# Dilated attention heads in three tiles of 128 partitions, with the instruction list drawn up anew

## The chip, the cores and the metric

The kernel runs on one core of a Trainium2 chip. The metric is the device time of one execution in microseconds (us). The engines are TensorE (PE; its weight loads are PEld), VectorE (DVE), ScalarE (ACT), GpSimd (POOL) and SyncE (SP, which issues all DMAs here).

## What is computed

Attention with eight heads of 64, four of them over a plain window of 32 keys and four over a dilated one (every fourth key, 32 of them), and on its result a feed-forward layer of 512 -> 2048 -> 512 with a gate. Cut to what matters:

```python
# q, k, v: (8, 8, 576, 64); w_in: (512, 2048), w_out: (2048, 512) in float64
rel = pos[:, None] - pos[None, :]
mask_plain = (rel >= 0) & (rel < 32)                        # heads 0 to 3
mask_dil = (rel >= 0) & (rel < 128) & (rel % 4 == 0)        # heads 4 to 7
scores = np.where(mask, q @ k.T / 8, -1e9)
attn = softmax(scores)
x = (attn @ v)                                              # -> (4608, 512)
h = x @ w_in
g = h * np.tanh(softplus(h))
return g @ w_out
```

## The kernel before

**Units.** The work is cut into 16 units of 288 tokens, half a sequence each (`u`, with `half`). A unit has two kinds of heads: kind 0 is plain, kind 1 dilated. Queries go in blocks of 32. Of kind 0 there are three tiles (`NB[0]`) of three blocks on 96 partitions (`QB`). Of kind 1 every residue modulo 4 has 72 queries, covered by three overlapping blocks, so there are four tiles of three blocks, one per residue. Keys of a block lie in a window of 64 (`WK`) or, in the first half of a sequence, 56 (`WD`).

**Steps of one unit.** `ld` loads q and keys, `qp` spreads the plain q on GpSimd, `lv` loads v (its dilated part `vd` in two or three transfers per half, each of which waits on SP for the one before), `sp` computes scores in PSUM (L577), `sc` masks and subtracts the row maximum on DVE (L598, L600, L609), `ex` is the exponential on ACT, `tp` splits the weights into two f16 parts and transposes them, `pr` finds the scale of v and splits it, `va` multiplies with v (L689), takes the denominators (`den`, ACT), their reciprocals (`rec`, DVE) and the quotient `xs` (L705), and `tx` splits `xs` into two f16 parts and transposes it into `x`. `va` and `tx` have three parts in a unit: 0 is kind 0, 1 and 2 are two tiles each of kind 1. Units 0 to 2 (`direct`) put the mask on by a matmul (L565) and transpose on PE (L659, L738); the others take a mask tile in SBUF and transpose by DMA.

**Feed-forward.** `ff` is the first product (L790, 128x288 matmuls, three passes of high and low parts), `gt`, `gq` and `ga` build the gated operand, `fo` (L972, units 0 to 2) and `fq` (L933, seven products instead of eight) are the second one.

**Weights.** They come as 64-bit numbers. `wl` loads a piece of 2 x 512 KB (ring `raw` of four buffers), `wm` copies the high words, `ww` makes f32 of the two words (POOL L411, DVE L413 and L415), `ws` finds the scale (PE L382 or L385, DVE), `wp` splits into two f16 parts (ACT L422, DVE L424). There are eight pieces of each matrix. `kw` and `kh` are matmuls on ones that fill PE early on.

**What sets the order.** The list `ORDER` is written out: each name calls the next part of a step, and its instructions are put on their engines in that order; `=n` names the PSUM buffer. Each engine runs its instructions in order, and SP its DMA issues. The small matmuls of the scores go round three column strips of 32 (`s`) and two row halves of 64 (`h`):

```python
        for t in range(nb):
            for a in range(2):
                for s in range(NS):
...
                    for h in range(2):
...
                        nc.tensor.matmul(pt[s * SQ:(s + 1) * SQ, h, c:c + w], q[hs, q0:q0 + SQ], d["k"][kind][hs, k0:k0 + w],
```

## Time and profile before

| | us |
|---|---|
| median of three runs | 858.7 (857.71 to 860.95) |
| the profiled execution | 862.81 |
| its span, first to last instruction | 860.9 |
| PE busy | 842.1 |
| DVE busy | 636.1 |
| ACT busy | 477.8 |
| POOL busy | 96.0 |

The page gives each engine's busy time as a share of the span. Matmuls are pipelined and their ends are modelled, so what a stretch of matmuls costs is read from the start of its first to the start of the next line. [...]

### The profile page before, as it was taken

To read this page: it belongs to the slowest core of one execution; us is meant where nothing else is said; L and a number is where in the kernel's file an instruction comes from. 1 tells how busy PE (TensorE), PEld (TensorE's weight loads), DVE (VectorE), ACT (ScalarE), POOL (GpSimd) and SP (SyncE) were. 2 spreads that over 40 slices of the span, in tenths; PEclk is the share of its full clock that TensorE was granted. 3 is DMA by queue.
4 is the path that set the end of the run, shared out by engine and by line. 5 is a ranking of instruction groups with operands and counts; after the bars stand their busy time and mean duration, and the time that the engine had idled before them with its cause. 6 is when DMAs were issued, how large, how long until landed. Compare 5 with 4: busy or idle time off the path is not lost.

```text
span 860.9 us, 32197 instructions
## 1 busy us (share of the span) xinstructions
PE 842.1 (98%) x14818; PEld 727.3 (84%) x14821; DVE 636.1 (74%) x818; ACT 477.8 (55%) x615; POOL 96.0 (11%) x99
## 2 busy tenths in 40 slices
PE   8798999999999999999999999999999999999998
PEld 7486777788788998988999889988889889988898
DVE  3788998586999897968777587977878764854353
ACT  2464655453486558765753775766446656624342
POOL 5116583210010001000000000010000000000000
PEclk9989999999999999999999999999999999999999
DMA  8648543366320437253623373725335160421001
GB/s 270 213 151 266 154 146 87 73 144 130 70 57 13 126 80 178 57 144 96 126 67 102 69 150 76 131 72 102 94 73 109 43 127 18 57 40 34 1 22 37
DMA packets 154887, 86.29 MB, mean 100 GB/s; under 512 B 92288, under 2 KB 150656, under 8 KB 154752
## 3 DMA queue, kind: packets, MB, share of 16 engines
q1 hardware_dynamic: 154752, 84.24, 40.9%
q8 instruction: 116, 1.90, 1.0%
q14 instruction: 19, 0.16, 0.1%
HBM read 56.89 MB, written 9.44 MB: 77 GB/s over the span
## 4 chain that ended last, share of the span: by engine, by line
PE 86%; DMA 7%; DVE 3%; SPq 2%; ACT 1%; issue 1%; POOL 0%; DVEq 0%; POOLq 0%; ACTq 0%
PE b L790 40%; PE b L933 31%; PE b L972 8%; DMA vf<-in_vd 4%; PE b L689 4%; PE b L577 3%; DMA raw<-in_w_in 2%; DMA knd<-in_kdT 1%; DVE g L903 1%; SPq L348 1%; DVE hm L909 0%; DVE w L424 0%; SPq L501 0%; PE b L385 0%; ACT g L901 0%
## 5 line engine op out<-in xcount | busy, mean ns | idle before, releaser
L790 PE MATMUL b<-x,w 128*128 128x288 f16 x3072 | 393.4, 286 | 0.2 <-ACT hm L796 0.2
L790 PEld LDWEIGHTS <-w 128*128 128x128 f16 x3072 | 295.4, 98 | 75.5 <-issue 0.6
L903 DVE SCALAR_TENSOR_TENSOR g<-hm,sg,g 128x1152 f16<-128x1152 f32 (+1 forms) x104 | 131.3, 1272 | 53.7 <-ACT g L901 52.9
L933 PE MATMUL b<-g,w 128*128 128x144 f16 x2496 | 164.9, 226 | 0.8 <-issue 0.7
L933 PEld LDWEIGHTS <-w 128*128 128x128 f16 x2496 | 158.4, 98 | 3.2 <-issue 1.1
L796 ACT ACTIVATE hm<-b,fs 128x576 f32<-128x576 f32 x128 | 92.8, 738 | 113.5 <-PE b L790 99.2
L901 ACT ACTIVATE g<-hm,sg 128x1152 f16<-128x1152 f32 (+1 forms) x104 | 116.0, 1127 | 40.1 <-PE b L933 26.4
L481 POOL COPY qp<-qn 128x576 f32<-128x576 f32 x15 | 34.9, 2326 | 433.6 <-DMA qn<-in_qT 317.9
L909 DVE TENSOR_TENSOR hm<-hm 128x576 f32<-128x576 f32 x104 | 79.0, 763 | 1.9 <-ACT hm L796 0.4
L972 PE MATMUL b<-g,w 128*128 128x288 f16 x576 | 73.3, 286 | 0.1
L947 ACT ACTIVATE y<-b,fo 128x288 f32<-128x288 f32 x52 | 40.6, 786 | 58.9 <-PE b L933 57.6
L972 PEld LDWEIGHTS <-w 128*128 128x128 f16 x576 | 55.6, 98 | 14.4 <-DVE w L424 0.3
L952 DVE SCALAR_TENSOR_TENSOR y<-b,fo,y 128x144 f32<-128x144 f32 x78 | 33.6, 478 | 45.8 <-PE b L933 22.7
L933 PE MATMUL b<-g,g 128*128 128x144 f16 x936 | 66.6, 226 | 0.3 <-DVE y L952 0.2
L933 PE MATMUL b<-g,late_sums 128*128 128x144 f16 x936 | 65.9, 226 | 0.0
L933 PEld LDWEIGHTS <-g 128*128 128x128 f16 x936 | 60.6, 98 | 2.2 <-issue 0.6
L933 PEld LDWEIGHTS <-late_sums 128*128 128x128 f16 x936 | 60.0, 98 | 0.5
L727 ACT CAST x<-xs 96x512 f16<-96x512 f32 (+1 forms) x39 | 26.7, 686 | 30.9 <-DMA x<-x 17.1
L729 DVE TENSOR_TENSOR x<-xs,x 96x512 f16<-96x512 f32 (+1 forms) x39 | 30.1, 772 | 16.6 <-ACT x L727 16.4
L545 DVE SCALAR_TENSOR_TENSOR vh<-vn,s,vh 128x2688 f16<-128x2688 f32 (+1 forms) x13 | 35.2, 2705 | 8.6 <-ACT vh L543 8.6
L705 DVE TENSOR_TENSOR xs<-b,rec 96x512 f32<-96x512 f32 (+1 forms) x48 | 37.2, 776 | 4.4 <-DVE rec L703 0.5
L689 PEld LDWEIGHTS <-pT 64*32 64x32 f16 (+1 forms) x3276 | 30.2, 90 | 5.3 <-issue 3.6
(127 smaller groups left out, 821.1 us busy)
## 6 DMA issues: line engine op xcount, KB each, us to landing
qn<-in_qT SPq DMA_DIRECT2D x15, 576.0 KB, 5.3
vn<-in_vd SPq DMA_DIRECT2D x66, 128.0 KB, 3.8
raw<-in_w_out SPq DMA_DIRECT2D x16, 512.0 KB, 5.2
out_T<-y SPq DMA_DIRECT2D x26, 288.0 KB, 2.8
raw<-in_w_in SPq DMA_DIRECT2D x12, 512.0 KB, 7.4
vn<-in_v SPq DMA_DIRECT2D x14, 288.0 KB, 4.2
knd<-in_kdT SPq DMA_DIRECT2D x14, 224.0 KB, 4.7
vn<-in_v SPq DMA_DIRECT2D x12, 256.0 KB, 3.7
```

The costliest lines, as they stand in the source:

```text
L481: nc.gpsimd.tensor_copy(qp.rearrange("p (b r i) -> p b r i", r=NR, i=SQ // NR), d["q"][:, :2 * HT].rearrange("p (b i r) -> p b r i", r=NR, ...
L545: nc.vector.scalar_tensor_tensor(lo, src, s, hi, ALU.mult, ALU.subtract)
L689: nc.tensor.matmul(avv[s * SQ:(s + 1) * SQ, a, t - t0, h * (D + 1):(h + 1) * (D + 1)], p, vv[vi][ks, v0:v0 + D + 1], start=(i == 0), stop= ...
L705: nc.vector.tensor_tensor(xs.rearrange("p (a t h e) -> p a t h e", a=2, h=2, e=D), avv[:, :, :, 1:AW - 1].rearrange("p a t (h e) -> p a t ...
L790: nc.tensor.matmul(ph[:, h, :HT], w1[j][:, c, wi, k * P:(k + 1) * P], x_of(d, xi, c), start=(n == 0), stop=(n == len(seq) - 1))
L796: nc.scalar.activation(d["m"][p][:, half, k0:k0 + 2], ph[:, :, :HT], AF.Mish, scale=d["fs"][:, j:j + 1])
L901: nc.scalar.activation(hi, src, AF.Identity, scale=sg)
L903: nc.vector.scalar_tensor_tensor(lo, src, sg, hi, ALU.mult, ALU.subtract)
L909: nc.vector.tensor_tensor(a, a, b, op=op)
L933: nc.tensor.matmul(acc[e], left(l, e, p, wi)[:, k * P:(k + 1) * P], right(gi, k), start=(n in opens and p == 0 and q == 0), stop=(last and ...
L947: nc.scalar.activation(into(half, t), by(acc), AF.Identity, scale=fo)
L972: nc.tensor.matmul(po[:, :HT], w2[:, e, j, wi, k * P:(k + 1) * P], d["g"][j][:, gi, k, :], start=(j == 0 and n == 0), stop=(j == NCH - 1 a ...
```

## The change

The dilated blocks are counted through all residues: block `j` of tile `t` is number `4 t + j`, and three tiles of four blocks lie on 128 partitions (`QS` is the number of rows of a tile, `NB` becomes 3 and 3). All rows of kind 1 then have 768 or 672 columns instead of 1024 or 896. `va` and `tx` have two parts in a unit, one per kind, so there is one `den`, `rec`, `xs`, one split and one transpose of kind 1 where there were two. The masks of kind 1 in units 3 to 15 come from SBUF tiles that `masks_late` makes by three more matmuls, since the pattern of a tile now differs from tile to tile; in units 0 to 2 the mask matmul is made per tile. GpSimd converts the weight words as before. The list `ORDER` is another one throughout (2030 names instead of 2123).

```diff
-    NB = (NPB, NR)
+    NB = (NPB, NR * NS * SQ // P)
+    QS = (QB, P)
...
+    def block(kind, t, j):
+
+        return divmod(t * P // SQ + j, NS) if kind else (t, j)
...
-                for s in range(NS):
-                    k0 = a * (NR * d["kd"] if kind else d["kw"]) + key_of(d, kind, t, s)
+                for j in range(nq // SQ):
+                    r, s = block(kind, t, j)
+                    k0 = a * (NR * d["kd"] if kind else d["kw"]) + key_of(d, kind, r, s)
...
-        src = pt[:QB, :, :n * WK].rearrange("p h (g k) -> p h g k", k=WK)[:, :, :, :w]
+        src = pt[:nq, :, :n * w].rearrange("p h (g k) -> p h g k", k=w)
...
-            nc.sync.dma_start_transpose(pT.rearrange("k (g q) -> k g q", q=QB), p16s[kind][:, :2 * n * P])
+            nc.sync.dma_start_transpose(pT.rearrange("k (g q) -> k g q", q=nq), p16s[kind][:, :2 * n * P])
...
-    def values(u, p):
+    def values(u, kind):
         d = U[u]
-        kind, t0, t1 = span(p)
...
-        for t in range(t0, t1):
+        for t in range(nb):
...
-            x16 = take("x16", x16s)[:, :4 * nt * P]
+            x16 = take("x16", x16s)[:nq, :4 * nb * P]
...
-ld0 ld0 wl0.3.0 lv0 mf cs0 qp0 ww0.3.0 xa0 cs1 wl0.3.1 xa1 kw18 kh32 sp0.0=0 wm0.3.0 ld0 mf lv0 ww0.3.0 ld0 wm0.3.0
...
+lv0 wl0.0.1 wl0.3.0 mf wm0.3.0 wm0.0.1 ld0 wl0.3.1 ld0 cs1 ww0.3.0 wl0.0.0 kw12 mf qp0 ld0 ww0.3.1 lv0 wm0.3.1 kh90
...
```

What this does to the order is shown at three places of the start. The first is SP's queue from its beginning. `raw` and `w_90` are pieces of w_in, `qn`/`knp`/`knd` q and keys of unit 0 (then 2), `qk` q and dilated keys of unit 1, `vf` v. Before:

```order
L466 DMA qn<-in_qT 128x1152
L471 DMA knp<-in_kT 128x2x288
L348 DMA raw<-in_w_in 128x512 x4
L475 DMA knd<-in_kdT 128x4x80
L501 DMA vf<-in_v 64x8x128
L475 DMA knd<-in_kdT 128x4x80
L348 DMA raw<-in_w_in 128x512 x4
L505 DMA vf<-in_vd 64x4x128 x2
L501 DMA vf<-in_v 64x8x128
L466 DMA qk<-in_qT 128x1152
L471 DMA knp<-in_kT 128x2x320
L475 DMA qk<-in_kdT 128x4x112 x2
```

After:

```order
L355 DMA raw<-in_w_in 128x512 x4
L473 DMA qn<-in_qT 128x1152
L355 DMA raw<-in_w_in 128x512 x2
L478 DMA knp<-in_kT 128x2x288
L355 DMA raw<-in_w_in 128x512 x2
L482 DMA knd<-in_kdT 128x4x80
L508 DMA vf<-in_v 64x8x128
L473 DMA qk<-in_qT 128x1152
L482 DMA knd<-in_kdT 128x4x80
L355 DMA w_90<-in_w_in 128x512 x2
L512 DMA vf<-in_vd 64x4x128 x2
L508 DMA vf<-in_v 64x8x128
```

Four weight transfers now stand ahead of unit 0's q, and two more of them and unit 1's q ahead of the first `vd` of unit 0; the dilated keys of unit 1 (`qk<-in_kdT`), which stood before the second `vd` pair, stand behind it.

The second place is DVE's queue where unit 0's `x` is made (`rec`, `xs`, low half of `x`; `w` and `raw` are weight words, `nm` row maxima). Before:

```order
L703 RECIPROCAL rec<-den 96x2x4
L705 TENSOR_TENSOR xs_681<-b_73,rec 96x512
L703 RECIPROCAL rec<-den 96x12
L705 TENSOR_TENSOR xs_699<-b_70,rec 96x768
L703 RECIPROCAL rec<-den 96x2x4
L705 TENSOR_TENSOR xs_703<-b_72,rec 96x512
L413 SCALAR_TENSOR_TENSOR w_87<-w_87,w_90 128x1024 x2
L746 TENSOR_TENSOR x<-b_73,x 128x2x192
L746 TENSOR_TENSOR x<-b_70,x 128x576
L746 TENSOR_TENSOR x<-b_71,x 128x2x192
```

After:

```order
L706 RECIPROCAL rec<-den 96x12
L708 TENSOR_TENSOR xs_658<-b_73,rec 96x768
L706 RECIPROCAL rec<-den 128x12
L708 TENSOR_TENSOR xs_728<-b_72,rec 128x768
L611 TENSOR_REDUCE nm<-b_70 128x12
L743 TENSOR_TENSOR x<-b_73,x 128x768
L743 TENSOR_TENSOR x<-b_71,x 128x576
```

Three rows of each sort have become two, the two weight rows have left the place between `xs` and `x`, and one row of maxima of unit 1 has come there.

The third place is PE's queue around unit 0's values (L689, later L695; `prep`'s maximum L330, later L337; fillers L999, later L996). Before:

```order
L604 MATMUL b_72<-nm,ident 96x512 x2
L689 MATMUL b_70<-vf,pp_417 32x65 x12
L330 LDWEIGHTS ones
L330 MATMUL b_73<-m_558,ones 128x2
L689 MATMUL b_70<-vf,pp_417 32x65 x12
L689 MATMUL b_73<-vf,pp_446 32x65 x12
L689 MATMUL b_70<-vf,pp_417 32x65 x12
L689 MATMUL b_73<-vf,pp_446 32x65 x12
L689 MATMUL b_72<-vf,pp_446 32x65 x24
L659 MATMUL b_71<-ident,sb 128x96 x8
```

After:

```order
L695 MATMUL b_72<-vf,pp_472 32x65 x32
L996 MATMUL b_73<-ones 128x96 x4
L695 MATMUL b_73<-vf,pp_433 32x65 x12
L695 MATMUL b_72<-vf,pp_472 32x65 x16
L337 LDWEIGHTS ones
L337 MATMUL b_70<-m_574,ones 128x2
L996 MATMUL b_73<-ones 128x96 x3
L695 MATMUL b_73<-vf,pp_433 32x65 x24
L996 MATMUL b_73<-ones 128x96 x2
```

The dilated values (`pp_472`) come first and in one buffer instead of two, with fillers between them and the plain ones.

## Rows read from the trace of the kernel before

**Rows 1.** The page's first part: busy us, share of span, instructions, by engine

```profile
PE 842.1 (98%) x14818; PEld 727.3 (84%) x14821; DVE 636.1 (74%) x818; ACT 477.8 (55%) x615; POOL 96.0 (11%) x99
```

**Rows 2.** PE's waits, 145.7 us to the end: releaser, us in total, times, longest

```profile
PE b L933 <- issue: 0.7, 1, 0.7
PE b L933 <- DVE y L952: 0.2, 1, 0.2
```

**Rows 3.** Busy PE, PEld, DVE, ACT, POOL (x); clock; DMA share, GB/s, by stretch

```profile
50.70:76.10 25.40, 22.65 (x350) 17.33 (x354) 21.61 (x34) 13.94 (x19) 6.40 (x5) 1.00 0.80 246
76.10:79.60 3.50, 3.50 (x105) 2.62 (x92) 2.53 (x3) 0.35 (x1) 1.32 (x2) 0.51 0.99 330
79.60:145.70 66.10, 63.94 (x861) 51.70 (x860) 60.44 (x84) 35.81 (x47) 42.64 (x19) 1.00 0.41 124
145.70:861.00 715.30, 710.22 (x12819) 622.86 (x12817) 521.45 (x657) 405.89 (x518) 28.66 (x36) 1.00 0.38 84
```

**Rows 4.** Timeline, PE and DVE at 42 to 51 us: start, us, instruction [idle before]

```profile
42.98 1.57 PE L689 MATMUL b<-vf,pp 64*32 64x65 f32 x73 [3.33 <-issue]
50.66 11.92 PE L790 MATMUL b<-x,w 128*128 128x288 f16 x96
...
47.31 2.35 DVE L413 SCALAR_TENSOR_TENSOR w<-w,w 128x1024 int32<-128x1024 int32 x2
```

**Rows 5.** PE's waits, 50.7 to 145.7 us, the longest three

```profile
PE b L577 <- DMA knd<-in_kdT: 1.8, 2, 1.4
PE b L382 <- DVE w L413: 0.9, 1, 0.9
PE b L577 <- DVE x L746: 0.8, 1, 0.8
```

**Rows 6.** DVE's groups by shape, 0 to 146 us: busy us, mean ns, idle before

```profile
L323 DVE TENSOR_REDUCE m<-vf 128x1 bf16<-128x1024 f32 x4 | 4.7, 1210 | 0.0
L705 DVE TENSOR_TENSOR xs<-b,rec 96x512 f32<-96x512 f32 x6 | 4.1, 687 | 0.8 <-PE b L738 0.3
L600 DVE TENSOR_REDUCE nm<-b 96x16 f32<-96x1024 f32 x3 | 3.7, 1221 | 3.6 <-PE b L577 3.6
L746 DVE TENSOR_TENSOR x<-b,x 128x384 f16<-128x384 f32 x6 | 3.3, 549 | 1.0 <-ACT x L744 1.0
L705 DVE TENSOR_TENSOR xs<-b,rec 96x768 f32<-96x768 f32 x3 | 2.9, 954 | 0.1
L600 DVE TENSOR_REDUCE nm<-b 96x12 f32<-96x768 f32 x3 | 2.9, 950 | 1.0 <-PE b L577 1.0
```

**Rows 7.** Timeline of PE, 657 to 680 us

```profile
657.28 1.38 PE L689 MATMUL b<-vh,pT 64*32 64x65 f16 x144
658.59 3.17 PE L933 MATMUL b<-g,late_sums 128*128 128x144 f16 x48
...
663.10 3.10 PE L790 MATMUL b<-x,w 128*128 128x288 f16 x24
666.04 1.66 PE L933 MATMUL b<-g,g 128*128 128x144 f16 x24
...
672.03 4.57 PE L790 MATMUL b<-x,w 128*128 128x288 f16 x36
676.54 0.97 PE L577 MATMUL b<-knp,qp 64*32 64x64 f32 x72
677.31 1.19 PE L577 MATMUL b<-knd,qn 64*32 64x64 f32 x96
678.43 1.76 PE L790 MATMUL b<-x,w 128*128 128x288 f16 x13
```

**Rows 8.** The chain that ended last, two of its pieces: start, us, what

```profile
44.74 2.75 DMA vf<-in_vd
...
84.63 0.33 PE b L738 x4
```

**Rows 9.** Timeline of SP's DMA issues, the second `vd` pair of unit 0

```profile
26.54 6.59 SPq L505 DMA_DIRECT2D vf<-in_vd  x2
```

More of the change, by code (lines that the diff above doesn't have):

```diff
@@ L619, in exps @@
         else:
-            nc.scalar.activation(x, x, AF.Exp, bias=ln_p[:QB])
+            nc.scalar.activation(x, x, AF.Exp, bias=ln_p[:QS[kind]])
     p16s, x16s, pTs = [], [], []
@@ L639, in transpose_p @@
         sb = d.pop(("sb", kind))
-        nb, w = NB[kind], width_of(d, kind)
+        nb, w, nq = NB[kind], width_of(d, kind), QS[kind]
         n = 2 * nb
@@ L752, in x_of @@
         kind, a = divmod(c, 2)
-        x = x_span(d, kind, 0, NB[kind])
+        x = x_span(d, kind)
+        at0 = (2 * i + a) * NB[kind] * QS[kind]
         if kind == 0:
-            at0 = (2 * i + a) * HT
             return x[:, at0:at0 + HT].rearrange("p (b r i) -> p r b i", r=NR, i=SQ // NR)
-        ap = x[:, (2 * i + a) * QB:]
-        return bass.AP(ap.tensor, ap.offset, [list(ap.ap[0]), [4 * QB, NR], [SQ + SD - DQ, NS], [1, SD]])
+        ap = x[:, at0:]
+        return bass.AP(ap.tensor, ap.offset, [list(ap.ap[0]), [NS * SQ, NR], [SQ + SD - DQ, NS], [1, SD]])
     def ff_scales(u, j=None):
```

402 lines of the change are left out of this document (198 added, 204 removed).

## The prediction

> **What bounds the kernel now.** I read the page's busy shares first, then TensorE's own waits by stretch, then the stretches' sums, and last single rows where a term is taken from. TensorE (PE) is busy for 842.1 of 860.9 us [rows 1]. From 145.7 us to the end it waits 0.9 us in all, the larger part being 0.7 us [rows 2], at full clock [rows 3]: in those 715 us only PE's own work counts, and whatever VectorE (DVE) or ScalarE save there is off the path. So the end moves by three things only: when the first feed-forward product starts (50.66 us [rows 4]), how long PE waits between 50.7 and 145.7 us (4.7 us, the largest parts in [rows 5]; in addition 3.5 us at the lower clock level, granted 0.51 [rows 3], which costs half of it, 1.75 us), and how much work PE has. In that second stretch DVE is busy 21.61 of 25.40 and 60.44 of 66.10 us [rows 3]; it prepares the weights, and two of the waits in [rows 5] are for it.
>
> **The change, part by part.**
>
> *Dilated tiles of 128 partitions.* Scores, values and the rest of the dilated half are the same arithmetic in 3 tiles of 128 rows instead of 4 of 96. An elementwise row costs by its columns: 1024 columns 1221 ns, 768 columns 950 ns [rows 6], on 96 partitions; 128 partitions cost no more, a maximum over 128 x 1024 takes 1210 ns [rows 6]. For the three units that run during start-up (0, 1, 2), DVE saves: maxima 3 x (1221-950) = 0.8 us; one subtraction of the maxima (unit 2) 0.27; `xs` 2 x 687 becomes one of 954, 3 x 0.42 = 1.26; the low half of x, 2 x 549 against about 950 for 768 columns, 3 x 0.15 = 0.45. Together 2.8 us. In units 3 to 15 the same saving (larger there, mask and P-low rows too) lies beside a PE that does not wait: nothing. If that cover were gone it would be worth about 2 us per unit to DVE, not to PE.
>
> *PE's small matmuls.* Their number stays (48 score and 144 value matmuls per unit); they now go round 4 column strips x 2 row halves instead of 3 x 2. What that is worth is bounded from both sides. 144 value matmuls of 65 columns take 1.31 us from their first to the next line's first [rows 7], 9.1 ns each. A 288-column f16 matmul takes 122.5 ns (24 of them 2.94 us, from 663.10 to 666.04 [rows 7]), so 65 columns stream in 28 ns and six at a time would allow 4.6 ns. The values are thus paced by their issue, at 9.1 ns, and a fourth strip gives nothing. The 96 score records take 1.12 us, 11.7 ns each [rows 7], slower than the issue pace, so there the strips do bind: at best they fall to 9.1 ns, 96 x 2.6 = 0.25 us per unit, 3.5 us in the 14 units whose scores come after the first feed-forward product; at worst 0. Half the units have 56-column keys and lie nearer the issue pace already, so I take 0.15 us per unit: **-2.1 us** (0 to -3.5). Transposes of `xs` in units 1 and 2 fall from 14 to 12, four of them take 0.33 us [rows 8]: **-0.3**.
>
> [...]
>
> *Groups.* Each visit to the small matmuls costs an entry: the 36 feed-forward matmuls ahead of the scores take 4.51 us to the next line, 4.41 by 122.5 ns [rows 7], 0.10 us; the exit has no row of its own, and I put it at half of that, 0.15 us in all. In the instruction order, after the first feed-forward product, there are 49 such groups before and 53 after: 4 x 0.15 = **+0.6**. The extra mask matmuls (three of 128 columns instead of one of 512) move no more columns: 0.
>
> *The start: first feed-forward product.* It needs all of unit 0's x, and that needs its last `vd` load. Each `vd` load waits on SyncE for the one before: the second pair holds SP 6.59 us [rows 9], and a lone one lands 2.75 us after its issue [rows 8]; so the last landed near 32.5 + 2.75 = 35.3 us. The new order puts 2 x 512 KB of w_in and a q of 576 KB ahead of the first `vd` of unit 0 that stood behind it, and takes 2 x 224 KB of keys of unit 1 from between: 1.18 MB more. At 246 GB/s [rows 3] that is 4.8 us; if DMA gaps take it up, 0. On the way from there to x, DVE did two weight rows of 2.35 us ahead of the low half of x [rows 4]; the new order has them behind it, -2.35; one `xs` less, -0.5; and PE stood 3.33 us in the value group for nothing that the profile names [rows 4]. That stall may be gone, or return at another place of the order. Ends: 0 - 2.85 - 3.3 = -6.2 us, and 4.8 - 2.85 = +1.9. Neither end is nearer to a row; I take the middle, **-2.1**. Nothing covers this term: PE has work without a break from 146 us on, so it goes to the end in full. SP holds behind these loads the rest of w_in and unit 1's v.
>
> [...]
>
> *50.7 to 145.7 us.* Of the 4.7 + 1.75 us lost there, 1.8 are for unit 2's `knd`, 0.9 in one piece for a weight row on DVE, 0.8 for `x` [rows 5]. DVE's 2.8 us less can remove the last two; the moved loads may remove the first and with it the low-clock stretch that followed it, or not. On the other hand a product that starts earlier meets weights that are not: by the sums of DVE rows up to the last weight split, the new order has the same weight work (17 word pairs, 16 splits) and four gate rows more ahead of it. Ends -5 and +3; I take **-1.0**.
>
> *145.7 us to the end.* The same feed-forward matmuls (8,016 in the whole program), the same kind of tail. DMA transposes of x fall from three to two per unit. But loads, prep and values stand closer together in the new list. Before, 0.9 us of waits; I take **+0.5** (0 to +4). GpSimd does the same conversions; its copy that spreads unit 0's q now stands behind the second half of the masks, covered as long as q and its keys land later still, which the order of the loads makes likely: 0.
>
> **The sum.** -2.1 - 0.3 + 0.6 - 2.1 - 1.0 + 0.5 = -4.4 us. The profiled execution took 862.81 us (its span 860.9 and 1.9 around it), so 858.4 of the same kind; that run lies 4.1 above the median of 858.7, which gives **854.3 us** as a median, 0.5% less. A measurement of this kernel can tell about 0.5% (4.3 us) from no change.
>
> **Rivals.**
> 1. *Nothing reaches the end.* The scores are paced by their issue like the values (0 instead of -2.1), and the start is ruled by bytes: 4.8 - 2.85 - 1.65 (half the stall) = +0.3 instead of -2.1. Then 854.3 + 2.1 + 2.4 = 858.8. For it: the 246 GB/s stand beside a DMA share of 0.80 [rows 3], so that little is left to take up more bytes; against: DVE's saving is certain.
> 2. *Slower: weights first starve unit 0 and unit 1.* If the last `vd` of unit 0 lands 5 us later and the 3.33 us stall comes back, the first product starts 1.9 us later than 50.66. SP then holds the last w_in piece, since its buffer is freed only after x of unit 0, and the six `vd` of unit 1, 2.75 us each, stand behind it; PE reaches unit 1's values after 144 products (18 us) and waits for them, say 4 us, and the low clock costs another 1.75. 854.3 + 4.0 + 1.0 (the gain of the next stretch) + 4 + 1.75 = 865. It decides from the point where the first product starts later than 50.66 us. For it: PE waited for `knd` here before [rows 5]; against: the second half of unit 1's v is needed 18 us after the first product, not at once.
> 3. *The start gains in full:* no later landing and no stall, -6.2 instead of -2.1: 850.2. For it: a list that is drawn up with x expected early; against: the bytes.
> [...]
> That the change does not do what it says is not open: the order shows 128-partition rows throughout.
>
> **How the numbers follow.** Forecast, 851 to 857 around 854.3: 0.45, of which half, 0.23, lies under 854.4 (the bound of 0.5%). Rival 1 (857 to 862): 0.20. Rival 2 (over 863): 0.17. Rival 3: 0.12. Rival 4: 0.06. Faster by over 0.5%: 0.23 + 0.12 + 0.06 = 0.41; within: 0.22 + 0.20 = 0.42; slower: 0.17. The range reaches from rival 4 to the foot of rival 2: 847.5 to 863, which leaves out rival 2's 0.17.
>
> **What would show it.** First feed-forward product between 44.5 and 53 us (forecast near 48.7); dilated score groups of 96 records near 0.97 us and value groups of 144 still near 1.3; DVE rows of 768 columns on 128 partitions at 0.95; PE's waits from 51 to 146 us under 4 us and after that under 2. I am wrong if the first product starts after 51 us, if PE waits for unit 1's v, or if waits of 5 us or more appear after 150 us.

## The result, and the profile after

The changed kernel takes **865.78 us** (median of four runs, 864.83 to 867.69), the kernel before 859.83 beside it (857.71 to 861.05): a ratio of 1.0073, 95% interval 1.0052 to 1.0093. It is slower by 0.7%, with the other sign than forecast and outside the range. The profiled executions took 867.69 and 862.81 us, 4.9 apart; this difference is what the two traces can explain.

The page's first part after the change, in the columns of [rows 1]:

```profile
PE 841.2 (97%) x14848; PEld 725.3 (84%) x14848; DVE 610.7 (71%) x770; ACT 458.1 (53%) x581; POOL 90.2 (10%) x99
```

The change did what it says: VectorE (DVE) is busy 25 us less than in [rows 1], ScalarE (ACT) 20 us less. TensorE (PE) has the work it had; its waits add up to 14.4 us in the trace before and 20.2 after. Where the 4.9 us lie is read from three points: the first feed-forward product, the end of the first 576 feed-forward matmuls (the start of the next one, 145.71 us before, the end of the first chunks), and the end of PE.

| | before | after | difference |
|---|---|---|---|
| first feed-forward product | 50.66 | 53.19 | +2.5 |
| end of the first 576 feed-forward matmuls | 145.71 | 144.98, with about 2.2 us of small matmuls still to do that before has done | +1.5 |
| end of PE's last matmul | 857.01 | 861.74 | +4.7 |

So 2.5 us are lost at the start, 1.0 gained to 145 us, and 3.2 lost after it. The stretches after the change (columns as in [rows 3]):

```profile
0.00:53.20 53.20, 40.73 (x728) 31.59 (x729) 28.29 (x41) 20.12 (x27) 20.32 (x39) 0.81 0.82 252
53.20:150.00 96.80, 92.54 (x1295) 73.58 (x1295) 85.18 (x110) 51.81 (x68) 47.86 (x20) 1.00 0.45 128
150.00:866.00 716.00, 707.92 (x12829) 620.12 (x12826) 497.23 (x621) 386.21 (x488) 22.00 (x40) 1.00 0.41 84
```

The granted clock (1.00 is full speed) of the first stretch is 0.81; TensorE was granted 0.50 for 20.5 us there, in three pieces: 10.2 us from 13.4 us, in a wait of PE of 3.41 us that ends at 14.32; 6.8 us from 33.9 us, behind waits of 1.59 and 1.31 us that end at 31.21 and 33.25; 3.4 us from 47.5 us, behind waits of 1.93 and 0.80 us that end at 45.61 and 47.17. From 53 us on it is at 1.00. PE's waits from 53.2 to 150 us, then from 150 us to the end (columns as in [rows 2]):

```profile
PE b L969 <- DVE m L538: 1.6, 1, 1.6
PE b L787 <- DVE w L431: 1.3, 1, 1.3
PE b L337 <- ACT pp L673: 0.6, 1, 0.6
PE b L787 <- DVE x L743: 0.4, 1, 0.4
...
PE b L337 <- DVE m L529: 1.6, 1, 1.6
PE b L930 <- DVE y L949: 1.0, 1, 1.0
PE b L695 <- DVE vh L552: 0.5, 1, 0.5
PE b L695 <- issue: 0.5, 1, 0.5
PE b L930 <- ACT y L944: 0.2, 1, 0.2
```

The wait for unit 2's `knd` of [rows 5] is gone, with the low clock behind it (0.51 for 3.5 us in [rows 3], 1.00 here). After 150 us there are 3.7 us where [rows 2] have 0.9; the largest, at 166 us, is unit 3's v, which lands later, so that its scale (L529) and the matmul of its maximum (L337) come late.

The start, PE's timeline from unit 0's values to the first feed-forward product (columns as in [rows 4]):

```profile
38.81 1.19 PE L695 MATMUL b<-vf,pp 64*32 64x65 f32 x64
39.94 1.48 PE L996 MATMUL b<-ones 128*128 128x96 f32 x8
41.34 0.81 PE L695 MATMUL b<-vf,pp 64*32 64x65 f32 x56
42.08 0.18 PE L337 MATMUL b<-m,ones 128*128 128x2 bf16 x1
...
45.61 0.66 PE L996 MATMUL b<-ones 128*128 128x96 f32 x4 [1.93 <-DVE rec L706]
46.10 0.28 PE L573 MATMUL b<-m_b,ident_b 96*128 96x128 bf16 x2
47.17 0.40 PE L573 MATMUL b<-m_b,ident_b 96*128 96x128 bf16 x4 [0.80 <-issue]
47.50 1.62 PE L593 MATMUL b<-qk 64*32 64x64 f32 x96
49.05 2.26 PE L737 MATMUL b<-ident,xs 96*128 96x96 f32 x12
...
53.19 4.78 PE L787 MATMUL b<-x,w 128*128 128x288 f16 x36
```

And DVE beside it:

```profile
37.01 2.34 DVE L330 TENSOR_REDUCE m<-vf 128x1 bf16<-128x1024 f32 x2
42.30 0.16 DVE L538 TENSOR_REDUCE m<-b 128x1 f32<-128x2 f32 x1 [2.95 <-PE b L337]
...
45.63 0.96 DVE L708 TENSOR_TENSOR xs<-b,rec 128x768 f32<-128x768 f32 x1
49.16 0.96 DVE L611 TENSOR_REDUCE nm<-b 128x12 f32<-128x768 f32 x1 [2.57 <-PE b L593]
52.18 0.96 DVE L743 TENSOR_TENSOR x<-b,x 128x768 f16<-128x768 f32 x1 [2.06 <-ACT x L741]
```

The maximum over v is done at 39.35 us, its matmul (L337) stands behind values and fillers and runs at 42.08; DVE waits 2.95 us for it, and the denominators, `rec` and `xs` follow. `xs` is ready at 46.59, 0.8 us earlier than before (47.39), but its transposes (L737) stand behind unit 1's dilated scores, which PE reaches late (1.93 us of a filler waiting for a buffer, 0.80 "issue") and works off at the lower clock: 49.05. So the time is lost behind `xs`: 6.60 us from there to the first product, where the kernel before took 3.27. There unit 1's dilated scores ran at 31.88 us, ahead of unit 0's values, and 3.33 us went into the stall of [rows 4].

Small matmuls, PE's timeline at 210 and 662 us:

```profile
210.93 1.17 PE L593 MATMUL b<-knd,qn 64*32 64x64 f32 x96
212.03 8.99 PE L969 MATMUL b<-g,w 128*128 128x288 f16 x72
...
662.28 1.35 PE L695 MATMUL b<-vh,pT 64*32 64x65 f16 x144
663.56 0.18 PE L337 MATMUL b<-m,ones 128*128 128x2 bf16 x1
```

96 scores take 1.10 us here (1.12 in [rows 7]), 144 values 1.28 (1.31). Over the groups of 96 scores that run without a break, the medians are 1.13 us before and 1.10 after with 64-column keys, and 1.06 in both with 56-column ones. The fourth strip brings next to nothing.

### The profile page after: what moved, and what is told of

It is laid out like the page before. It is cut to its first block, busy times and chain, and to the rows that moved or that the text cites. A ratio compares the mean times of both kernels' runs of the same rounds, so it can differ in the third digit from the quotient of the medians.

```text
span 865.8 us, 32135 instructions
## 1 busy us (share of the span) xinstructions
PE 841.2 (97%) x14848; PEld 725.3 (84%) x14848; DVE 610.7 (71%) x770; ACT 458.1 (53%) x581; POOL 90.2 (10%) x99
## 4 chain that ended last, share of the span: by engine, by line
PE 82%; DMA 7%; DVE 6%; SPq 2%; issue 1%; ACT 1%; POOL 1%; DVEq 0%; ACTq 0%; POOLq 0%
PE b L787 37%; PE b L930 30%; PE b L969 7%; PE b L695 4%; PE b L593 3%; DMA vf<-in_vd 2%; DMA raw<-in_w_in 2%; DMA vn<-in_vd 1%; DVE w L431 1%; DVE raw L422 1%; DMA raw<-in_w_out 1%; DVE w L420 1%; SPq L512 1%; DVE g L900 1%; POOL raw L418 1%
## 5 line engine op out<-in xcount | busy, mean ns | idle before, releaser
L900 DVE SCALAR_TENSOR_TENSOR g<-hm,sg,g 128x1152 f16<-128x1152 f32 (+1 forms) x104 | 131.7, 1278 | 61.5 <-ACT g L898 61.3
L930 PE MATMUL b<-g,w 128*128 128x144 f16 x2496 | 167.1, 226 | 0.1
L488 POOL COPY qp<-qn 128x576 f32<-128x576 f32 x15 | 21.5, 1433 | 395.4 <-DMA qn<-in_qT 250.0
L695 PEld LDWEIGHTS <-pT 64*32 64x32 f16 (+1 forms) x3276 | 29.6, 89 | 7.6 <-issue 5.8
L609 DVE SCALAR_TENSOR_TENSOR sb<-b,m_p 96x768 f32<-96x768 f32 (+2 forms) x26 | 24.2, 929 | 16.1 <-PE b L593 11.4
L695 PE MATMUL b<-vh,pT 64*32 64x65 f16 (+1 forms) x3276 | 34.2, 196 | 1.0 <-DVE vh L552 0.5
L730 DVE TENSOR_TENSOR x<-xs,x 96x768 f16<-96x768 f32 (+1 forms) x26 | 24.7, 950 | 12.1 <-ACT x L728 12.1
```

Of the source, the lines that this page charges most:

```text
L695: nc.tensor.matmul(avv[j * SQ:(j + 1) * SQ, a, t, h * (D + 1):(h + 1) * (D + 1)], p, vv[vi][ks, v0:v0 + D + 1], start=(i == 0), stop=(i == ...
L900: nc.vector.scalar_tensor_tensor(lo, src, sg, hi, ALU.mult, ALU.subtract)
L930: nc.tensor.matmul(acc[e], left(l, e, p, wi)[:, k * P:(k + 1) * P], right(gi, k), start=(n in opens and p == 0 and q == 0), stop=(last and ...
```

## Experiments

The list `ORDER` is the object of most of them; a diff shows the names that move. Ratios are to the kernel before on the same chip, with 95% intervals; where a first product or an end of PE is given, it is from that kernel's one trace. How much such a value scatters is seen where two kernels below have the same list up to 100 us: the changed kernel and g2 have their first product at 53.19 and 51.61 us, g1 and g3 at 50.24 and 51.79. So a difference of 1.6 us between two traces of the start is not yet an effect of an edit.

### The new tiles on the old list

```diff
-ORDER of the changed kernel
+ORDER of before; of the two dilated parts of va and tx in a unit the earlier is dropped
```

> The new tiles (three of four blocks on 128 partitions) put into the list of the kernel before: of the two parts that each unit's dilated values and transposes had there, the earlier one is dropped and the later one does all three tiles; the masks of units 3 to 15 take one step more. Nothing else of the list is moved, no load above all. Theory START (the loss of the changed kernel comes from the new list's first 53 us, where the first feed-forward product falls at 53.19 us instead of 50.66, and from its waits of 1 to 2 us later): first product at 50 to 51 us, dilated score groups of 96 near 1.08 us instead of 1.13 as in the changed kernel, time 857 to 860. Theory TILES (the 128-partition tiles themselves cost: four strips, mask matmuls by tile, one larger x step that comes later): 863 to 867, with the loss spread over all units. Theory LATER (part of the old order rests on dilated values in two steps, so that x comes later with one): first product near 50.7 but waits for x behind it, 860 to 863.

Measured: 881.15 us, ratio 1.0261 (1.0229 to 1.0293). The first product comes at 46.59, 4.1 us earlier than before, so the tiles by themselves do not make the start longer. But then PE waits (whole program):

```profile
PE b L695 <- issue: 14.1, 6, 4.8
PE b L593 <- issue: 5.0, 3, 1.9
PE b L930 <- issue: 3.2, 3, 1.4
```

22 us of "issue", waits for nothing the profile names, most of them in values and scores (7.5 us in the kernel before). This was unexpected, and none of the three theories had it; "Where the issue stalls come from" below takes it up.

### The order at the start

`e2` puts unit 1's scores behind unit 0's transposes, `e3` the maximum's matmul ahead of values and fillers, `e4` both. `g1` does it differently: without the 18 filler records and with weight splits behind `xs`.

```diff
e2
-sp1.1=0 ww0.2.0 sp1.1 ... sc1.1 tx0.0=1 lv1 tx0.1=3 tx0.0 ... tx0.0
+ww0.2.0 ... tx0.0=1 lv1 tx0.1=3 sp1.1=0 sp1.1 tx0.0 ... tx0.0 sc1.1 sc1.1
e3
-pr0 pr0 kw4 va0.0=3 va0.1 pr0=0 kw3 pr0 va0.0 ... va0.0 kw2 ex1.0
+pr0 pr0 pr0=0 pr0 va0.0=3 va0.1 va0.0 ... va0.0 kw9 ex1.0
g1
+pr0 pr0 pr0=0 pr0 va0.0=3 va0.1 va0.0 ... sp1.1=0 sp1.1 sc1.1 wp0.0.0 fs0.0 tx0.0=1
```

> The changed kernel with one move in its list: unit 1's dilated scores (two steps) and their maxima go behind the transposes of unit 0's xs, which they preceded. In the changed kernel xs is ready at 46.59 us, but the transposes start at 49.05, behind four mask and 96 score matmuls. Theory START: transposes near 46.9 us, first feed-forward product 2 us earlier, near 51.0, and all of it reaches the end: 863 to 864. Theory TILES: the start doesn't matter, 865 to 867. Theory GIVEN BACK (the start is earlier, but the products then wait for weight splits on VectorE, which one already does for 1.3 us at 59.26): first product near 51, waits after it up by 1.5 to 2 us, time 865 to 866.

> The changed kernel with one move in its list: the small matmul that spreads the maximum of unit 0's v over the partitions goes ahead of the values, and the 14 filler matmuls (two steps of four and three f32 ones) that stood between the parts of the values go behind them. In the changed kernel VectorE has that maximum at 39.35 us and waits 2.95 us for the matmul at 42.08; the values end at 43.68. Theory START: eps at about 40 us instead of 43.0, values end near 41.5, xs done at 44.5 instead of 46.6, first feed-forward product near 51 (unit 1's scores still ahead of the transposes): 863 to 864. Rival: x is bound by what else VectorE has in its queue (a weight split of 1.27 us ahead of the reciprocals), first product later than 52.5, 865 to 866. With fewer fillers between, the clock may stay at half for longer: then the 20.5 us at half of the changed kernel grow, and the gain is under 1 us.

> The changed kernel with both moves, unit 0's prep matmul ahead of its values (fillers behind them) and unit 1's dilated scores behind the transposes of unit 0's xs. Theory START: the gains add, first feed-forward product at 48.5 to 49.5 us, 861 to 862, still above the kernel before by the later waits (8.5 us in the feed-forward rows after the first product against 3.7). Theory GIVEN BACK: the products then wait for the weight splits behind them: first product near 49, waits between it and 100 us up by 2 us or more, 863 to 865. Theory TILES: 865 to 867.

> The changed kernel with its list altered between unit 0's values and its first feed-forward product: the matmul that spreads the maximum of v goes behind the second of the six value steps, the 18 filler records between and behind the values are left out, the weight split goes behind both xs, and the transposes of xs follow unit 1's dilated scores directly, with the loads' and weight steps that stood between moved behind them. All of unit 1's scores stay ahead of the first product, as in the changed kernel (the two runs before that moved them or kept fillers there did not start earlier: first products at 55.55, 53.39 and 57.95 us). Theory START: last vd at 36.5 us, eps near 41, xs done near 44 instead of 46.6, first product at 47 to 49 us instead of 53.2 with the same work done before it, time 860 to 862. Theory GIVEN BACK (loads set the pace: unit 1's last vd landed at 72.5 us): the product starts early, but PE waits later for unit 1's v or for weight words; waits between the first product and 100 us grow by 3 us or more, 864 to 866. Theory FETCH (PE's own instructions come in blocks of about 128 matmul records over a DMA queue, and a block's transfer of 1 to 1.2 us begins only when bulk loads have drained: in the changed kernel the block of record 605 is transferred from 44.06 to 45.40 us and PE stands still until 47.17): with 18 records fewer the boundary falls behind the transposes of xs, so no stall if those come after 46 us, otherwise up to 2 us.

Measured: e2 868.60 (ratio 1.0108, 1.0076 to 1.0140), e3 865.57 (1.0073, 1.0046 to 1.0100), e4 866.81 (1.0091, 1.0062 to 1.0120), g1 867.21 (1.0098, 1.0074 to 1.0122). None is better. In e2 the transposes run 1.6 us earlier, but the scores' maxima now stand ahead of the products: PE waits 1.97 us for them and starts at 55.55. In e3 L337 runs 0.9 us earlier, and the fillers behind the values wait 2.02 us for DVE's `rec`, then take 3.7 us, 18 of them 0.20 us each (0.14 at the full clock, by six from 42.12 us in the changed kernel), so by my estimate most of it at the lower clock: 53.39. In e4 both moves together give 57.95. g1 starts at 50.24, and shows why it is not earlier (PE's timeline):

```profile
40.50 0.34 PE L593 MATMUL b<-qk 64*32 64x64 f32 x14
43.59 1.49 PE L593 MATMUL b<-qk 64*32 64x64 f32 x82 [2.76 <-issue]
```

The stall of [rows 4] is back, in another line.

### The two later waits

```diff
-tp3.1 pr3=3 ld4 qp4 tp3.0 pr3 ff2.6=2 fo0.3.0 ff2.6
+tp3.1 ld4 qp4 tp3.0 ff2.6=2 fo0.3.0 ff2.6 pr3=3 pr3
-fo0.0.0=1 va2.1=3 va2.1
+va2.1=3 va2.1 fo0.0.0=1
```

> The changed kernel with two later moves only, nothing before 100 us touched: unit 3's matmul that spreads the maximum of v goes behind two half groups of products (it waited 1.77 us at 166 us for a v that landed late), and the first product of the second matrix goes behind two parts of unit 2's values (it waited 1.81 us at 113.3 us for VectorE). Theory LATER WAITS (what PE waits after the first product reaches the end one to one): these two waits vanish, 862 to 863. Rival: each wait only moves to the next instruction that needs the same VectorE result, 865 to 866.

> Both of the foregoing edits together, the new start and the two later moves. If START and LATER WAITS hold, their gains add: 857 to 859, level with the kernel before. If the earlier start is given back to loads, as g2_later, 862 to 863. If neither, 865 to 866.

> The changed kernel with both sets of list edits: the two later moves of the earlier run, and a start in which PE does nothing but unit 0 between its values and its first product: prep matmul behind the second value step, fillers left out, xs transposed directly, unit 1's dilated scores behind the transposes, their maxima behind the first twelve products. In the two runs with the foregoing form of this start, PE stood still for 2.76 and 3.5 us inside unit 1's scores, at matmul record 604 of the program, waiting for its own next block of instructions (transferred from 41.17 to 42.09 us); now that record is reached only after the transposes. Theory START: first product at 46 to 48 us without that stall, 5 to 6 us earlier than in the changed kernel, and most of it reaches the end: 858 to 860. Theory GIVEN BACK (behind the first product VectorE, 22.75 of 25.40 us and 22.03 of 23.90 us busy there in the changed kernel, and the loads set the pace, not PE's start): first product as early as that, but waits behind it up by 4 us or more, 863 to 866.

Measured: g2 864.45 (12 runs; 1.0055, 1.0038 to 1.0071), g3 (g1's start with it) 866.95 (1.0080, 1.0056 to 1.0103), h1 (scores behind transposes, no fillers, and g2's moves) 864.90 (1.0058, 1.0038 to 1.0077). g2's trace no longer has the 1.6 us for v at 166 us; the one at 113 us is 1.5 now, for ACT. Its median is 1.3 us below the changed kernel's, which its interval does not tell from nothing. h1 has its first product at 47.42 us, 5.8 earlier than the changed kernel, and its PE ends at 855.78, 6.0 earlier, in a trace that is of the fastest of its nine runs (861.95 to 867.29). The median moves by 0.9. So a start as early as was forecast does not by itself give the forecast time.

### VectorE's work

The operation that puts the sign into the low words of the weights is done on an eighth of the columns for 12 of the 16 weight pieces, so the weights' low parts are not the reference's.

```diff
-scalar_tensor_tensor(lo[:, c], hi[:, c], -0x80000000, a[:, c], ...)
+n = CH // 8 if k or g in (1, 2) else CH
+scalar_tensor_tensor(lo[:, c, :n], hi[:, c, :n], -0x80000000, a[:, c, :n], ...)
```

> The changed kernel, list untouched, with VectorE relieved: the operation that puts the sign into the low words of the weights is done on 128 of 1024 columns for 12 of the 16 pieces (all of the second matrix, the middle ones of the first), so the rest of these words is left wrong. It takes 1.21 us each time now and should take 0.2 to 0.3, 11 to 12 us less of VectorE's work between 53 and 130 us. Theory GIVEN BACK TO VECTORE: PE's waits for VectorE's results behind the first product (1.46 us at 57.7, 0.5 at 85.8, 1.81 at 113.3 and the 0.8 before it) vanish or halve, 861 to 863; the wait at 166 us for a load stays. Rival LOADS (these results are late because the words' loads are): the waits stay, 865 to 866.

> The early start and the two later moves together with the relieved VectorE of the run before (low words of 12 weight pieces left wrong in 7 of 8 columns). Theory GIVEN BACK TO VECTORE: with VectorE relieved the early start does reach the end, first product at 46 to 48 us, waits behind it 3 us or less, 854 to 857. If loads set the pace, the start is given back all the same: 861 to 864.

> The kernel before, list and tiles untouched, with VectorE relieved in the same way (low words of 12 weight pieces left wrong in 7 of 8 columns). VectorE is less busy there behind the first product, 21.65 of 25.44 and 19.96 of 23.90 us. Theory GIVEN BACK TO VECTORE, in the form that the changed kernel is bound by VectorE there and the kernel before is not: 858 to 859, no change, or at most the two waits for weight words of 0.9 and 0.7 us, 857. If it gains as much as the changed kernel does from the same relief (3 us or more), VectorE is no difference between the two.

Measured: on the changed kernel 862.34 (h2), on h1 861.19 (h3), on the kernel before **856.14** (h4; ratio 0.9966, 0.9951 to 0.9981). The relief is worth 3.3 to 3.7 us in each; in the traces of h2 and h4 the first product comes at 48.31 and 48.33 us, 4.9 and 2.3 earlier than without it. So DVE's weight work is a bound of the start and the first chunks in both kernels, which is not what tells them apart: the gap between h2 and h4 is 6.2 us, as between the kernels themselves (5.95).

### The loads, and the kernel before without its stall

`f1` puts unit 1's first `vd` loads ahead of four weight transfers in the kernel before; `f2` in addition moves ACT's and DVE's steps on those weights behind unit 0's first products. PE's records stay as many as in the kernel before. Their order stays in f1; in f2, other than its expectation says, three scale matmuls (L382, step `ws`) go from ahead of the first product to behind 48 products.

```diff
f1
-lv1 wp0.0.1 wl0.1.0 tp0.0 ... va0.2=2 lv1 va0.2 lv1 va0.0
+lv1 lv1 wp0.0.1 wl0.1.0 tp0.0 ... va0.2=2 va0.2 lv1 va0.0
f2, on top
-wl0.2.1 wm0.1.0 ... wm0.1.1 ... ww0.1.0 ... ww0.1.1 ... ww0.1.1 ... ws0.1=2 ... ff0.6=3 ff0.6
+wl0.2.1 ... wp0.0.1 wm0.1.0 wm0.1.1 ww0.1.1 ff0.6=3 ff0.6 ww0.1.0 ww0.1.1 ff0.7=0 ff0.0=1 ws0.1=2
```

> The kernel before (old tiles, old list) with one move among its loads: unit 1's first three dilated v loads of 128 KB go ahead of four weight pieces of 512 KB that were issued just before unit 0's values. In the kernel before PE stood still for 3.33 us inside those values (39.65 to 42.98 us), where the trace shows a 16 KB block of instructions being transferred from 40.17 to 41.21 us, while the DMA engines were 0.98 busy until 41.2. Theory FETCH: the v loads wait for one another, so the DMA engines are nearly idle around 38 to 41 us, the block comes early, the stall falls from 3.33 to under 1 us, first feed-forward product near 47.5 instead of 50.66 us; time 855 to 857, or 858 to 860 if the four weight pieces then come too late for the third and fourth pair of products. Rival (the stall has another cause, in the values themselves): stall still 3.3 us, first product at 50.5, time 858 to 860.

> Edit: the kernel before, unit 1's first v loads ahead of four 512 KB weight pieces (as in f1_loads_behind_v) and the weight steps that used to run on ScalarE and VectorE ahead of unit 0's x moved behind its first feed-forward products; TensorE's records are as many and in the same order as before. Theory LOADS: the 3.33 us stall ahead of the fifth group of value products [rows 4] was a fetch of TensorE's own instructions behind bulk loads, and f1 lost its gain only because a ScalarE copy of a denominator stood queued behind a weight copy. Then the first feed-forward product is at 46.5 to 47.5 and the time 854 to 857, or 858 to 860 if the later weights take it back. Rival START IS PAID LATER: the first product comes earlier, the time is 859 or more because the weights moved late are waited for in the second and third chunk.

Measured: f1 864.77 (1.0060, 1.0038 to 1.0081), f2 861.54 (12 runs; 1.0024, 1.0011 to 1.0037). f1's PE, then its ACT:

```profile
37.37 0.99 PE L689 MATMUL b<-vf,pp 64*32 64x65 f32 x73 [0.31 <-issue]
...
47.63 1.20 PE L659 MATMUL b<-ident,sb 96*128 96x96 f32 x6 [6.45 <-DVE xs L705]
53.59 0.68 PE L790 MATMUL b<-x,w 128*128 128x288 f16 x2
...
45.09 1.13 ACT L370 ACTIVATE w<-w 128x1024 f32<-128x1024 f32 x1 [6.83 <-DMA w<-in_w_in]
46.11 0.35 ACT L697 ACTIVATE den<-b,eps,f 96x8 f32<-96x8 f32 x1
```

The 3.33 us stall of [rows 4] has shrunk to 0.31, at the same matmul. In its place a denominator stands on ACT behind a weight copy (L370) that waits 6.83 us for the weights which now land later, and the first product comes at 53.59 instead of the 47.5 forecast. f2 removes that: it shows no such wait, and its first product is at 47.58, 3.1 us earlier than before, in part because L382 no longer stands ahead of it. At the 192nd feed-forward matmul 2.1 us of that lead are left, at the 576th 1.6, at PE's end 2.4 (854.65 against 857.01). Yet its median is 1.8 us longer than that of the kernel before, whose trace is of an execution 3 us above its median. The rival recorded for f2, that the start is paid back later, stands on the time; the trace shows only a part of the lead paid back.

### The clock of the start

`c1` puts 105 filler records into the gaps of unit 0's small work, `c2` 155 more (into buffers that are free just then), for which 14 longer ones go.

```diff
c1
-kh90 ... ww0.0.1 sc0.0
+kh150 ... ww0.0.1 kh45 sc0.0
c2, on top
-tp0.1=3 sp1.0=1 ... tp0.1 kw3 ... sc1.0 kw2 sc1.0 ... va0.0 kw2 ex1.0
+tp0.1=3 kh35=2 sp1.0=1 ... tp0.1 kh40=2 ... sc1.0 kh40=2 sc1.0 ... va0.0 kh40=0 ex1.0
```

> The changed kernel with 105 more short filler matmuls (ones in bf16, nothing reads them) in two gaps of PE: 60 ahead of unit 0's first scores, where PE waited 3.41 us for keys (10.9 to 14.3 us), and 45 behind them, where it waited 2.42 us for the row maximum (15.8 to 18.3 us). Theory CLOCK: what the changed kernel loses is TensorE's clock. Its mean granted clock is 0.988 in all four executions on record, that of the kernel before 0.994 to 0.998 in most; of its trace's first 53 us the clock stands at half in 13.4 to 23.6, 33.9 to 40.7 and 47.5 to 50.9 us, each time after PE had waited 1.9 to 5.8 us shortly before. With these two gaps filled the stretch from 13.4 to 23.6 us runs at full clock, mean clock near 0.993; the small f32 matmuls of that stretch and what hangs on them take 3 us less; time 861 to 864. Rival START BOUND BY LOADS (unit 0's last v at 36.5 us sets x whatever PE does before): mean clock up, time unchanged, 864 to 866. Rival: the fillers only delay PE, 866 to 869.

> As the run before, and the other gaps of the first 48 us filled as well: the three places where f32 fillers waited for another engine because their PSUM bank was in use (1.31, 1.93 us and a shorter one) get short bf16 fillers into a free bank, and 35 stand where PE waited 1.59 us for unit 1's keys. Theory CLOCK: at half only up to about 7 us, mean clock 0.994 to 0.996 as in the kernel before, first feed-forward product 2 to 4 us earlier than 53.2, time 858 to 861. If START BOUND BY LOADS: mean clock up, time 863 to 866.

Measured: c1 867.47 (1.0098, 1.0077 to 1.0118), c2 865.20 (1.0066, 1.0049 to 1.0084). c2's stretch to the first product:

```profile
0.00:53.40 53.40, 46.82 (x973) 39.43 (x974) 28.96 (x41) 20.11 (x27) 20.70 (x39) 0.94 0.79 252
```

A granted clock of 0.94 there where the changed kernel has 0.81, and 0.996 over the run where it has 0.988, and the first product is still at 53.41. So in these two traces the lower level goes with PE's waits (46.82 us busy at 0.94, 40.73 at 0.81), and it is not shown to make the start long. The test is not quite clean: c2's records also shift the boundaries described in the next part, and its start has 1.9 us of "issue" waits where the changed kernel has 0.8. At the end the higher clock brings nothing that can be told from no change (865.20 and 865.78).

### Where the issue stalls come from

The profile's part on DMA queues has a queue of its own for instructions: in the changed kernel

```profile
q8 instruction: 116, 1.90, 0.9%
```

116 transfers of 1.90 MB, 16 KB each; PE has 14,848 matmuls and as many weight loads, 256 for each transfer. Setting the transfers of that queue beside PE's "issue" stalls gives the following (matmuls counted from the program's start, to about 2):

```
kernel   matmuls before   stall, us           transfer on the instruction queue, us
before     222            16.35 to 18.30      15.73 to 16.84
before     477            33.08 to 34.38      31.54 to 32.78
before     603            39.65 to 42.98      40.17 to 41.21
after      605            46.37 to 47.17      44.06 to 45.40
e1         604            37.20 to 40.52      37.91 to 38.94
e1        1111            75.55 to 80.39      77.90 to 79.05
g1         604            40.83 to 43.59      41.17 to 42.09
f1         603            37.06 to 37.37      34.59 to 35.93
c3        2646           183.58 to 184.57    182.23 to 183.31
c3        2902           195.48 to 196.59    194.21 to 195.09
```

The stalls stand at the same counts in kernels whose lines there differ, 126 to 128 matmuls or a multiple apart, and each ends 1.3 to 1.8 us after a transfer does. The profile names no cause; from these counts and times I take it that PE waits there, at a boundary of 128 matmuls, for its own instructions. 128 products of 122.5 ns last 15.7 us, 128 small matmuls of 9.1 to 11.7 ns 1.2 to 1.5; a transfer takes 0.9 to 2.2 us in the trace of before and 0.9 to 1.7 in that of after (median 1.1 and 1.0). In e1 the one of 77.90 us began 2.35 us after the stall had, while the DMA engines moved 338 to 386 GB/s. It does not have to wait until bulk loads have drained, as g1's theory has it: the one of 40.17 to 41.21 us in the kernel before ran while the DMA engines were full (a share of 1.03 and 404 GB/s from 39.65 to 41.21). The stall at 39.65 us lies in a stretch (34.3 to 42.9 us) with a DMA share of 0.91; f1, which moves loads alone and leaves PE's records as they are, has 0.31 us left of it at the same count.

`c3` moves the boundaries of the kernel before and nothing else of its work, by taking 34 filler matmuls out ahead of unit 0's dilated scores:

```diff
-ww0.3.1 kw17 sp0.1=1
+ww0.3.1 sp0.1=1
```

> The kernel before with one group of fillers left out: the 34 filler records that PE runs from 11.1 to 15.0 us, while it has nothing else to do (unit 0's dilated keys come at 15 us). Theory CLOCK: PE stands idle there for 4 us as the changed kernel does at the same place, the clock falls to half for 5 to 10 us more, mean clock 0.990 or less instead of 0.996, time 862 to 865 instead of 859.4. Rival START BOUND BY LOADS: clock lower, time 859 to 860.

Measured: 880.71 us, ratio 1.0235 (1.0209 to 1.0260): 21 us longer, for 34 small matmuls less, which neither of the two theories had. Its first product comes earlier (48.54). The boundary at about 222 matmuls lies in unit 0's dilated scores in both kernels, behind 44 of them in the kernel before and behind 78 in c3, 34 more. Its PE waits, and the same 180 value matmuls in c3 and in the kernel before:

```profile
PE b L689 <- issue: 10.1, 8, 3.2
PE b L577 <- issue: 8.2, 8, 1.5
```

```profile
182.21 1.37 PE L689 MATMUL b<-vh,pT 64*32 64x65 f16 x146
184.57 0.43 PE L689 MATMUL b<-vh,pT 64*32 64x65 f16 x34 [0.99 <-issue]
```

```profile
184.09 1.68 PE L689 MATMUL b<-vh,pT 64*32 64x65 f16 x180
```

In c3 a boundary falls into the group and PE stands 0.99 us; in the kernel before it does not. The stretches between c3's stalls have 256, 255 and 1278 matmuls (PE's busy time, clock, DMA share, GB/s):

```profile
172.70:184.50 11.80, 10.84 (x256) 1.00 0.71 190
184.50:196.50 12.00, 10.91 (x255) 1.00 0.19 53
196.50:287.20 90.70, 89.34 (x1278) 1.00 0.30 73
```

From its first product to PE's end c3 takes 822.3 us, the kernel before 806.4: 15.9 more, and its "issue" waits there are 15.5 us more (16.2 against 0.7). So they are what c3's trace loses. The two traces differ by 13.8 us at PE's end; the rest of the 21 us between the medians is not explained by them.

The list of the changed kernel has only 1.3 us of such stalls in the whole trace, that of before 7.5 (6.8 of them ahead of the first product). In the main e1's 881 us are a shift of this kind too: 22 of the 33 us of waits in its trace are "issue". From first product to PE's end it takes 26.6 us longer than the kernel before: 15.1 us are "issue" waits, about 7 come from 17.1 us at the lower clock (3.4 before; granted 0.89 from 55 to 100 us, 0.99 from 150 to 400), most of it right behind such stalls, and 4.6 are other waits. Without the first two PE would end at 857.7 us, against 857.0 before. By this estimate from two traces the tiles on the old list cost nothing and gain nothing.

Every edit of the start had also shifted all later boundaries: h1 by 18 matmuls, c1 by 105, whose trace has 4.1 us of "issue" waits after the first product where the changed kernel has 0.5. `i1` is h1 with 22 fillers put back in a free buffer, `i2` adds c1's fillers and 23 more, in all a block and 4 more than the changed kernel.

```diff
i1, on h1
-va0.0 va0.0 va0.1 ex1.0
+va0.0 va0.0 va0.1 kh22=0 ex1.0
```

> Edit: h1_start_later plus 22 records of the filler product into a free bank between unit 0's dilated values and its transposes, so that all later records of TensorE stand within 4 of where the changed kernel has them (h1 has 18 fewer). Theory ALIGNMENT: TensorE's instructions come in blocks of 128 records, and a block whose predecessor holds many 10 ns records is waited for; h1 shifted the boundaries into groups of values and scores. With the shift taken back the stalls in the value rows after the first product (1.63 us at 447 in h1) are gone and the time is 859 to 863, against 864.9 of h1. Rival: boundaries shifted by 18 cost nothing in sum, 864 to 866.

> Edit: i1 plus the fillers of c1 (105 records in the gaps of unit 0's small work) and 23 more ahead of unit 1's scores, 132 records over the changed kernel in all, which is one block of 128 and 4. Theory ALIGNMENT AND CLOCK: c1 lost its gain in clock to boundaries that it shifted by 105; with them back in place the mean granted clock is 0.993 or more and the time 858 to 861. Rival: the clock of the start brings nothing at the end, the time is that of i1 within 1 us.

Measured: 864.21 (1.0060, 1.0042 to 1.0077) and 864.22 (1.0056, 1.0039 to 1.0074). The largest of PE's "issue" waits after the first product, h1's and then i1's:

```profile
PE b L695 <- issue: 1.6, 1, 1.6
```

```profile
PE b L787 <- issue: 0.4, 1, 0.4
PE b L695 <- issue: 0.3, 1, 0.3
```

The stall in the values goes as the theory has it, and from first product to end i1 takes 805.8 us, h1 808.4. But i1's extra fillers run into a boundary at the start, where the block came behind the loads:

```profile
47.02 0.25 PE L996 MATMUL b<-ones 128*128 128x96 bf16 x2 [4.52 <-issue]
```

Its first product is 3.9 us later than h1's, and the time as the rival said. i2 has a mean clock of 0.991 and the same time; its trace, too, has such a stall at the start (3.50 us, to 45.69). So neither shows what the boundaries alone are worth.

## Why the prediction was wrong

**The start (-2.1 forecast, +2.5 measured) is the step that failed.** Its two ends were -6.2 and +1.9, and the middle was taken; the measured value lies above both. The term took single rows (the stall, two weight rows, one `xs`) off the old chain from v to the first product, and left the order of the other steps as it had been. The traces show this in its place:

- The bytes ahead of the last `vd` cost less than the 4.8 us put down: it landed at 36.53 against 35.18, 1.35 later.
- Of the 3.33 us stall 0.80 came back at the same count of matmuls.
- The matmul of v's maximum (L337), which ran at once behind that maximum in the kernel before (as L330, 38.44 us), now stood behind values and fillers, and DVE waited 2.95 us for it.
- The transposes of `xs` now stood behind 96 scores of unit 1, which had run ahead of unit 0's values. With them and the lower clock, the way from `xs` to the first product took 3.3 us more.
- The two weight rows of 2.35 us were not on the path. In the kernel before PE went from the transposes through L382 into the first product at 50.66 us without waiting for DVE, whose rows of the low half of `x` ran until 51.25 (columns as in [rows 4]):

```profile
48.80 0.52 PE L738 MATMUL b<-ident,xs 96*128 96x96 f32 x4
49.76 1.06 PE L382 MATMUL b<-w,ones 128*128 128x512 bf16 x3 [0.44 <-ACT pp L662]
49.57 1.68 DVE L746 TENSOR_TENSOR x<-b,x 128x384 f16<-128x384 f32 x3
```

I had read from the order that two weight rows left the place between `xs` and `x`, and not that the transposes now stood behind 96 scores, nor that L337 stood behind fillers. The second is in the excerpt of PE's queue quoted ahead of the prediction. I also had the stall down as one for nothing that the profile names. The times of the instruction queue's transfers point to what it was: where PE's work is small matmuls, the stalls set beside them above last 0.3 to 4.8 us each. The size +2.5 is from one trace; by g2's start it would be +1.0, and neither shows the gain of 2.1. That the start goes to the end in full was a premise too, and the medians do not bear it out: h1's first product is 5.8 us earlier than the changed kernel's, its median 0.9.

**Scores (-2.1 forecast).** 0.03 us per group of 96 with 64-column keys and nothing with 56-column ones, which is half of the 14 units: -0.2. The bound of 9.1 ns was wrong for them: 11.5 ns a matmul after, 11.7 before. **Values (0)** went right, 9.1 to 8.9 ns. No run shows what rival 4's 0.06 and the range's lower end of 847.5 stand on, scores and values both shrunk to 6/8 by the fourth strip: they went from 11.7 to 11.5 and from 9.1 to 8.9 ns a matmul, and rival 4 is out.

**Groups (+0.6)** can't be read apart from the rest: PE's time after the first product without its waits is 800.7 us in both traces, of which 3.5 us before ran at the lower clock. The **transposes (-0.3)** of units 1 and 2 are 24 instead of 28, but take 2.55 us instead of 2.38.

**50.7 to 145.7 us (-1.0):** 1.0 gained, in part by luck. The wait for `knd` and its low clock went, but DVE's saving, which was to remove waits for DVE, did not: waits for DVE's weights (1.3) and for DVE's `m` (1.6) came.

**After 145.7 us (+0.5, with scores and groups -1.0):** +3.2, of which 2.8 are waits: mostly unit 3's v, and `y`. The bound of +4 held, the value did not. DVE's saving is off the path there, as said.

**DVE rows, GpSimd's copy:** right. 768 columns on 128 partitions take 0.96 us, and q was spread at 13.4 us while its keys landed at 14.2.

**Rivals.** Rival 2's time (865) came out, and its deciding point (a first product later than 50.66) was passed, but not its mechanism: the last `vd` of unit 0 landed 1.35 us later and not 5, and PE did not wait for unit 1's v, though the last of it landed at 72.54 us instead of 61.59. So its time came out by luck. What the traces show is a chain on the order of PE's own steps, which no rival named. Of what would show me wrong, a first product after 51 us is what happened.

**What stays open.** The traces place 4.7 of 4.9 us between two executions; that these places are the cause of the 6 us between the medians is not shown. They don't say why mending each place (start in h1, the later waits in g2, the clock in c2, boundaries in i1) gave at most 1.6 us of 6 in the medians. One relation might point on: over 89 runs of the kernel before the time falls by 4.8 us for each 0.01 of mean clock (correlation -0.66), whose median there is 0.995; the changed kernel has 0.988, h1, g2 and i1 0.986. That would be 3.4 to 4.3 us. But c2, at 0.996, is no faster, so that it is not the clock of the start, and for later stretches at the lower level in executions that were not profiled there is no trace. Not tried was the run that would tell the tiles from the list: e1 with fillers that put its boundaries back where the kernel before has them. No version tried beats the kernel before with its full work; h4, which leaves work out, shows where a gain would lie: DVE's weight words in the first 145 us.

## What to carry to other kernels

Read PE's "issue" stalls against the count of its matmuls: where they stand at multiples of 128, each edit that adds or removes matmuls shifts all later stalls, and a filler that looks free may be what keeps boundaries out of the runs of small matmuls (here 34 fillers less made 21 us more). When a new order makes a chain's data earlier, check what stands ahead of each of its steps on every queue, step by step, before the gain is put down. And when single executions of a kernel scatter by 3 us, two traces can place 5 us but not prove where the median's 6 went.

## What was not expected of the hardware

Removing 34 filler matmuls from a program of 14,800 made it 21 us longer (c3). A block of instructions was waited for up to 4.84 us (e1, from 75.55 us), where its transfer started only at 77.90 us, with the DMA engines moving 338 to 386 GB/s until then. And 96 score matmuls on four column strips instead of three take 11.5 ns each instead of 11.7, so the strips were not what paced them.
